# First batch's softmax turned by TensorE through PSUM, with a new order in the opening, and four side units moved

## The chip, the cores and the metric

The kernel runs on one core of a Trainium2 chip. Its time is the device time of one execution in microseconds (us), and the kernel before has a median of 645.45 us over three runs (644.94 to 646.62). Five engines work side by side, each through its own instructions in order: TensorE (PE, matrix products into the eight banks of PSUM, with its weight loads shown as PEld), VectorE (DVE), ScalarE (ACT), GpSimd (POOL) and SyncE (SP), which issues most transfers.

## The reference

Attention in both directions between 512 tokens and 32 state rows per head (8 batches, 8 heads, 64 wide), then one feed-forward layer over all 4,608 rows:

```
scores = x @ state.T / 8 ;  a  = softmax(scores)  ;  xread = a @ state    (tokens read the state)
scores2 = state @ x.T / 8 ; a2 = softmax(scores2) ;  sread = a2 @ x           (state reads the tokens)
X = rows of [xread, sread], 512 wide (8 heads x 64)
h = X @ w_in (512 x 2048) ;  g = h - tanh(h) ;  out = g @ w_out (2048 x 512)
```

The two weights arrive as 64-bit floats, and the kernel makes 32-bit ones of them itself.

## The kernel before

**Folding.** xread is never formed. For each batch the kernel builds M = (the states of 8 heads) times w_in, which is 256 x 2048, so that h = a M: per slice f of 128 columns of w_in there is a "hidden" product into a PSUM bank `hps`, tanh on ACT, the difference on DVE, and the "output" product into four banks `ops` (one per 128 tokens). Batches are called chunks, 0 to 7; chunk 8 is sread. A main loop of 64 steps (one step is one slice f of one of chunks 0 to 3, hidden two steps ahead) lets `ASIDE`, a table of step numbers, hang side work on the steps: `"att3"` is the attention of batch 3 in pieces, `"m0"` runs `m_units`, whose 16 units build M for batches 2 to 7. Batch 0's outputs are made in two halves: the first half's sums are stored and read back at step 29 as four tiles `part0` to `part3` (`load_partial`), and added at step 31, the end of chunk 0, by four DVE adds, `ob` (L587).

**The ring c2.** Tiles with the tag `c2` share four slots in turn: the copies `sl` that each unit of `m_units` makes and sends out by four transfers (`late`, L249), the four `part` tiles, and the last two of the four `ob` tiles of a chunk's store (`tag, bufs = ... ("c2", CSB)`). Who gets a slot waits until its last holder has been read.

**The opening.** Chunk 0 cannot start before its softmax, its M and its weights are there. This first stretch is written out by hand as a string of letters, `SEQ`; each becomes instructions, and each engine keeps this order. The digit is a half j of batch 0 (512 columns) or a weight block. S: scores (PE, bank `sps`). c: copy to `s` (ACT). T: turn to tokens on partitions. M, B, E, Z, N: maximum, subtraction (DVE), exponential (ACT), sum, division (DVE). A: turn back, giving `at`. Between them the weights are converted: a, b (DVE), r (ACT), p (DVE) turn a 64-bit block into 32-bit values. m: M's product (PE, bank `mps`). k and R: the copies (ACT) of the two halves of `mps`, for batch 0 (`m_first`) and batch 1 (`m_second`). h and H: the two halves of a hidden product (PE). X, x: tanh and difference. D: a product of zeros (`warm <- blank`) whose result nobody reads. In the kernel before, T and A are DVE transposes in blocks of 32x32.

After `SEQ` a scheduler sets the order on each engine from the order of the code and its own costs. Blocks 4 and 5 of the weights are rows 0 and 1 of w_out (r4, r5, p4, p5); after p5 DVE converts w10, w11, w02, w12 and w13 and splits row 2 of w_out into a high and a low part (L104, `wo`); PE needs the low part for the products of L566.

Of the kernel before, what the change touches and what calls it, by code (L numbers as in the profile page):

```python
# [9 lines left out]
F32 = mybir.dt.float32  # L10
# [6 lines left out]
AX = mybir.AxisListType  # L17
# [3 lines left out]
P = 128  # L21
B, H, S, NS, D = 8, 8, 512, 32, 64
# [16 lines left out]
def attention_ffn(ctx: ExitStack, tc: tile.TileContext, xT, xn, bd, bh, sp, sm, sl, win, wout, xout, tout, sout):  # L39
# [10 lines left out]
    nc = tc.nc  # L50

    cpool = ctx.enter_context(tc.tile_pool(name="cpool", bufs=1))
    pool = ctx.enter_context(tc.tile_pool(name="pool", bufs=2))
    dram = ctx.enter_context(tc.tile_pool(name="dram", bufs=1, space=DRAM))
    ps_o = ctx.enter_context(tc.tile_pool(name="ps_o", bufs=4, space=PSUM))
# [12 lines left out]
    TB = int('3')  # L68
    RRB = int('1')
    PTB = int('2')  # L70
    ident = cpool.tile([P, P], F32, name="ident")
    make_identity(nc, ident)
    wo = {}
    wod = dram.tile([P, 2, 2, NFF // 2, 2, 256], F32, name="wod")
# [13 lines left out]
    def bank(p, name):  # L88
        return p.tile([P, 512], F32, tag=p.name, name=name)
# [7 lines left out]
    def big(name, shape, dtype):  # L97
        return pool.tile(shape, dtype, tag="big", name=name, bufs=BIG)
# [7 lines left out]
    class Weight:  # L106
# [5 lines left out]
        def load(self):  # L112
            if self.src.dtype == F32:
                self.raw = next(raws)(f"{self.name}d", [P, 512], F32)
                dst = self.raw
            else:
                self.raw = next(raws)(f"{self.name}d", [P, 512, 2], U32)
                dst = self.raw.rearrange("p f w -> p (f w)")
            src = self.src.bitcast(dst.dtype)
            if len(src.shape) == 3:  # L120
                dst = dst.rearrange("p (r f) -> p r f", r=4)
            loadlog.append(nc.sync.dma_start(dst, src).ins)
# [19 lines left out]
        def convert(self, dst):  # L142
            return [step() for step in self.steps(dst)][1].ins
# [14 lines left out]
    def second(q):  # L158
        return pool.tile([P, 2, 512], F32, tag="stage", name=f"mr1{q}", bufs=SB)
# [438 lines left out]
    ats = [None] * 2  # L598
# [53 lines left out]
    def o(x):  # L652
        tc.keep_in_program_order(x)
        if x.ins.engine == mybir.EngineType.DVE:
            firstDVE[0] = x.ins
# [9 lines left out]
    nc.sync.dma_start(sps, sp)  # L665
    load(3)

    blank = pool.tile([P, 512], F32, tag="t", name="blank", bufs=TB)
    nc.gpsimd.memset(blank, 0.0)
    warm = bank(ps_a, "warm")  # L670
    m_first[0] = pool.tile([P, 2, 512], F32, tag="mr", name="mr00", bufs=RRB)
    wb, mps, sps_ps, hps, ss = {}, {}, {}, {}, {}
    es, ms, zs = {}, {}, {}
    csteps = {}
    hts = {}
    PING = int('0')
# [3 lines left out]
    def e3(hf):  # L680
        return es[hf].rearrange("p (a n) -> p a n", n=32)

    def step(op):
        k, j = op[0], int(op[1]) if len(op) > 1 else 0
        if k == "D":
            o(nc.tensor.matmul(warm[:, :256], blank[:, :P], blank[:, :256], start=True, stop=True))
        elif k == "S":
            sps_ps[j] = bank(ps_o, f"sps0{j}")
            for c in range(2):
                o(nc.tensor.matmul(sps_ps[j][64 * c : 64 * c + 64], bdr[:, 2 * j + c], xrs[j][:, c], start=True, stop=True))  # L690
        elif k == "c":
            if j == 0:
                kept[0] = pool.tile([P, 2, 512], F32, tag="g", name="s0", bufs=GB)
            ss[j] = kept[0][:, j]
            o(nc.scalar.copy(ss[j], sps_ps[j]))
        elif k == "T":
            es[j] = pool.tile([P, 512], F32, tag="e", name=f"e0{j}")
            o(nc.vector.transpose(es[j], ss[j]))
        elif k == "M":
            ms[j] = pool.tile([P, 16, 1], F32, tag="m1", name=f"m10{j}")  # L700
            o(nc.vector.reduce_max(ms[j], e3(j), axis=AX.X))
        elif k == "B":
            o(nc.vector.tensor_sub(e3(j), e3(j), ms[j].broadcast_to([P, 16, 32])))
        elif k == "E":
            o(nc.scalar.activation(es[j], es[j], AF.Exp, scale=SCALE))
        elif k == "Z":
            zs[j] = pool.tile([P, 16, 1], F32, tag="z", name=f"z0{j}")
            o(nc.vector.reduce_sum(zs[j], e3(j), axis=AX.X))
            o(nc.vector.tensor_scalar_add(zs[j], zs[j], EPS))
            o(nc.vector.reciprocal(zs[j], zs[j]))  # L710
        elif k == "N":
            o(nc.vector.tensor_mul(e3(j), e3(j), zs[j].broadcast_to([P, 16, 32])))
        elif k == "A":
            ats[j] = pool.tile([P, 512], F32, tag="p2t", name=f"at0{j}", bufs=PTB)
            o(nc.vector.transpose(ats[j], es[j]))
        elif k in "abrp":
            if j not in csteps:
                if j > 3:
                    if j == 4:
                        plain[0] = big("wp0", [P, 2, DM], F32)  # L720
                    csteps[j] = wos[j - 4].steps(plain[0][:, j - 4])
                else:
                    if j % 2 == 0:
                        wb[j // 2] = pool.tile([P, 2, 512], F32, tag="wf", name=f"w00{j}", bufs=WB)
                    csteps[j] = w0[0][j].steps(wb[j // 2][:, j % 2])
            o(csteps[j]["abrp".index(k)]())
            if k == "p":
                load(1)
            if k == "p" and j < 4:
                w = wb[j // 2][:, j % 2].rearrange("p (r f) -> p r f", r=4)  # L730
                nc.sync.dma_start(wf[0][:, :, j * P : j * P + P], w)
        elif k == "m":
            w = wb[j // 2][:, j % 2].rearrange("p (r f) -> p r f", r=4)
            mps[j] = bank(MP[j], f"mps0{j}").rearrange("p (r f) -> p r f", r=4)
            for p in range(4):
                o(nc.tensor.matmul(mps[j][:, p], sps[:, p], w[:, p], start=True, stop=True))
        elif k == "k":
            for c in range(2):
                o(nc.scalar.copy(m_first[0][64 * c : 64 * c + 64, :, j * P : j * P + P], mps[j][0:64, c::2]))
        elif k in "hH":  # L740
            if k == "h":
                hps[j] = bank(ps_h, f"hps0_{j}")
            i = "hH".index(k)
            o(nc.tensor.matmul(hps[j], m_first[0][:, i, j * P : j * P + P], ats[i], start=(i == 0), stop=(i == 1)))
        elif k == "X":
            t = hts[j] = pool.tile([P, 512], F32, tag="t", name=f"t0_{j}", bufs=TB)
            hts[j, 0] = nc.scalar.activation(t, hps[j], AF.Tanh)
            o(hts[j, 0])
        elif k == "x":
            g = chunks[0].g[j] = pool.tile([P, 512], F32, tag="g", name=f"g0_{j}", bufs=GB)  # L750
            d = nc.vector.tensor_sub(g, hps[j], hts[j])
            o(d)
            tanhs.append((hts[j, 0].ins, d.ins))
        elif k == "R":

            if 0 not in m_second:
                m_second[0] = second(0)
            for c in range(2):
                o(nc.scalar.copy(m_second[0][64 * c : 64 * c + 64, :, j * P : j * P + P], mps[j][64:128, c::2]))

    MP = [{"a": ps_a, "o": ps_o}[x] for x in 'oaoa']
    SEQ = 'S0 a0 c0 r0 b0 D D S1 T0 p0 M0 m0 a1 c1 B0 E0 T1 r1 b1 M1 k0 p1 D D D m1 B1 k1 r2 Z0 a2 N0 b2 D D D A0 E1 Z1 h0 p2 N1 R0 h1 A1 r4 r3 m2 R1 a3 H0 b3 k2 X0 H1 X1 p3 m3 x0 k3 R3 a4 x1 b4 R2 p4 a5 r5 b5 p5'
    for op in SEQ.split():
        step(op)
    chunks[0].m[0] = [m_first[0][:, k] for k in range(2)], None
    a0 = state_read(0, ss)
    late1 = late_read(1)
    turn = firstDVE[0]
    for p in range(2):
# [6 lines left out]
    m1 = m_units()  # L776
# [4 lines left out]
        "first": [18],  # L781
        "att2": [17, 18, 19, 22, 23, 25, 26, 27, 28],
        "part": [29],
        "m0": [17, 18, 19, 20, 22, 23, 24, 25, 26, 27, 28, 29, 30, 31, 33, 34],
        "att3": [29, 30, 30, 31, 32, 33, 34, 35, 36],
        "a0": [37, 38, 38, 39],
        "att5": [39, 40, 40, 41, 42, 43, 44, 45, 46],
# [262 lines left out]
    for n, duo in enumerate(duos):  # L1050
        a, b = duo.a.i, duo.b.i
# [112 lines left out]
```

## Time and profile before

| | us |
|---|---|
| median of three runs | 645.45 (644.94 to 646.62) |
| the profiled execution, whole | 646.61 |
| its span, first to last instruction | 644.8 |
| PE busy | 630.7 (98%) |
| DVE busy | 474.9 (74%) |
| ACT busy | 386.5 (60%) |

A span is what the profiler saw; the device time has 1.8 us around it. PE is busy nearly all the time, so time can be won or lost mainly where PE stands still, and the rows further down are of these places. A product of two 32-bit operands is two records on PE, so "x4" may be two products.

### The profile page before, as it was taken

The numbers are of one execution on the slowest core, as the hardware profiler recorded it, in microseconds if no ns is written. First come the engines' busy times: TensorE is split into PE (matmuls) and PEld (weight loads), VectorE is DVE, ScalarE is ACT, GpSimd is POOL, SyncE is SP. The second block draws the span as 40 slices with busy tenths as digits, with TensorE's granted clock in tenths as the row PEclk, the third lists the DMA queues.
The fourth block names the chain that finished last, engine by engine and source line by source line (L and its number), as shares of the span: only waits on it lengthen the run. The fifth ranks groups of instructions, "written<-read, shape, count | busy, mean of one in ns | idle before, by whom it ended". The sixth has DMA issues, their size and how long they took to land.

```text
span 644.8 us, 9604 instructions
## 1 busy us (share of the span) xinstructions
PE 630.7 (98%) x3448; PEld 485.8 (75%) x3448; DVE 474.9 (74%) x769; ACT 386.5 (60%) x667; POOL 24.4 (4%) x39
## 2 busy tenths in 40 slices
PE   6999999999998999999999999999999999999997
PEld 3445777777775788778878887788888888888996
DVE  5989998577556975999439777997955789754542
ACT  4874899668666765676546675456655553543432
POOL 0000000000000000000000000000000000333300
PEclk9999999999999999999999999999999999999999
DMA  9993964768897866679951446474565536999800
GB/s 316 293 372 119 350 201 174 221 159 280 264 292 239 291 215 213 209 241 350 384 210 36 161 132 228 136 228 156 169 177 165 189 113 188 301 319 340 274 23 33
DMA packets 67439, 141.21 MB, mean 219 GB/s; under 512 B 6976, under 2 KB 28736, under 8 KB 67392
## 3 DMA queue, kind: packets, MB, share of 16 engines
q1 hardware_dynamic: 64688, 132.08, 62.5%
q0 software_dynamic: 2560, 8.39, 3.8%
q8 instruction: 27, 0.44, 0.3%
q14 instruction: 20, 0.16, 0.1%
q10 hardware_dynamic: 144, 0.13, 0.1%
HBM read 96.01 MB, written 44.56 MB: 218 GB/s over the span
## 4 chain that ended last, share of the span: by engine, by line
PE 90%; DVE 3%; DMA 3%; ACT 1%; SPq 1%; issue 1%; DVEq 0%; ACTq 0%
PE X L999 13%; PE hps L509 10%; PE ops L565 9%; PE hps L510 9%; PE ops L567 9%; PE hps L511 9%; PE ops L566 9%; PE Y1m L999 5%; PE Y0m L999 4%; PE ops L563 2%; PE mps L240 2%; PE mls L247 2%; PE rps L455 1%; DMA w01d<-in_win 1%; PE hps L507 1%; PE pps L434 1%
## 5 line engine op out<-in xcount | busy, mean ns | idle before, releaser
L509 PE MATMUL hps<-aT,m 128*128 128x512 f32 x240 | 95.9, 402 | 0.3 <-DVE G L524 0.2
L510 PE MATMUL hps<-aT,m 128*128 128x512 f32 x240 | 93.8, 391 | 0.0
L511 PE MATMUL hps<-aT,m 128*128 128x512 f32 x240 | 93.4, 390 | 0.0
L565 PE MATMUL ops<-wo,g 128*128 128x512 f32 x232 | 91.1, 397 | 1.7 <-DVE ob L587 1.7
L566 PE MATMUL ops<-wo,g 128*128 128x512 f32 x232 | 90.7, 391 | 0.6 <-DVE wo L104 0.6
L567 PE MATMUL ops<-wo,g 128*128 128x512 f32 x232 | 84.5, 393 | 0.0
L530 DVE TENSOR_TENSOR t<-hps,t 128x512 f32<-128x512 f32 (+1 forms) x74 | 46.6, 630 | 39.6 <-ACT t L530 39.0
L524 ACT ACTIVATE t<-hps 128x512 f32<-128x512 f32 x64 | 38.3, 598 | 62.5 <-PE hps L511 60.0
L524 DVE TENSOR_TENSOR G<-hps,t 128x512 f32<-128x512 f32 x64 | 43.9, 687 | 36.4 <-ACT t L524 36.3
L530 ACT ACTIVATE t<-hps 128x512 f32<-128x512 f32 (+1 forms) x74 | 40.8, 551 | 46.0 <-PE hps L511 45.4
L104 ACT CAST g<-t 128x512 fp32r<-128x512 f32 (+1 forms) x74 | 42.4, 574 | 27.2 <-DVE t L530 26.9
L104 DVE TENSOR_TENSOR g<-t,g 128x512 fp32r<-128x512 f32 (+1 forms) x74 | 46.7, 631 | 16.0 <-ACT g L104 15.8
L565 PEld LDWEIGHTS ops<-wo,g 128*128 128x128 f32 x232 | 43.4, 188 | 18.8 <-DVE ob L587 2.2
L509 PEld LDWEIGHTS hps<-aT,m 128*128 128x128 f32 x240 | 45.1, 188 | 15.0 <-DVE G L524 2.1
L511 PEld LDWEIGHTS hps<-aT,m 128*128 128x128 f32 x240 | 45.1, 188 | 9.5
L510 PEld LDWEIGHTS hps<-aT,m 128*128 128x128 f32 x240 | 45.1, 188 | 9.1 <-issue 0.2
L566 PEld LDWEIGHTS ops<-wo,g 128*128 128x128 f32 x232 | 43.6, 188 | 10.6 <-DVE wo L104 1.0
L567 PEld LDWEIGHTS ops<-wo,g 128*128 128x128 f32 x232 | 43.2, 188 | 11.0 <-DVE wo L104 0.8
L999 PE MATMUL X<-g0m,W0m 128*128 128x512 f32 x192 | 46.6, 389 | 0.0
L104 ACT CAST g1m<-G 128x1024 fp32r<-128x1024 f32 x28 | 29.5, 1056 | 28.0 <-PE Y1m L999 11.9
L1037 POOL DMA_DIRECT2D wl<-wod x32 | 23.3, 728 | 587.7 <-DMA W1m<-wsd 556.6
L999 PE MATMUL X<-g1m,W1m 128*128 128x512 f32 x192 | 45.3, 389 | 0.0
(263 smaller groups left out, 1159.0 us busy)
## 6 DMA issues: line engine op xcount, KB each, us to landing
mr<-md SPq DMA_DIRECT2D x26, 512.0 KB, 4.0
xT<-in_xT SPq DMA_DIRECT2D x16, 512.0 KB, 6.1
md<-st SPq DMA_DIRECT2D x64, 128.0 KB, 2.6
xn<-in_xn SPq DMA_DIRECT2D x16, 512.0 KB, 5.6
wsd<-ws SPq DMA_DIRECT2D x16, 512.0 KB, 4.2
wod<-wo SPq DMA_DIRECT2D x32, 256.0 KB, 6.1
W0m<-wsd SPq DMA_DIRECT2D x16, 512.0 KB, 3.8
W1m<-wsd SPq DMA_DIRECT2D x16, 512.0 KB, 4.3
```

What stands on the lines that cost most here:

```text
L104: return nc.scalar.copy(hi, src), (sub or nc.vector).tensor_sub(lo, src, hi)
L240: made = nc.tensor.matmul(pss[e], s0[rows, x, 2 * p + e], t[rows, y], start=(n == 0), stop=(n == 2))
L509: nc.tensor.matmul(ps, mhi[k][:, cols], ahi[:, k], start=(k == 0), stop=False)
L510: nc.tensor.matmul(ps, mhi[k][:, cols], alo[:, k], start=False, stop=False)
L511: made = nc.tensor.matmul(ps, mlo[k][:, cols], ahi[:, k], start=False, stop=(k == nk - 1))
L524: main(nc.scalar.activation(t, ps, AF.Tanh), nc.vector.tensor_sub(g, ps, t))
L530: tanhs.append((nc.scalar.activation(t, ps, AF.Tanh).ins, nc.vector.tensor_sub(t, ps, t).ins))
L565: nc.tensor.matmul(o, g[:, 0, tok], w[:, 0], start=(f in self.begins), stop=False)
L566: nc.tensor.matmul(o, g[:, 0, tok], w[:, 1], start=False, stop=False)
L567: return nc.tensor.matmul(o, g[:, 1, tok], w[:, 0], start=False, stop=stop).ins
L999: made = nc.tensor.matmul(out[t], w[:, e, x, cols], y[:, e], start=first and j == 0 and e == 0 and c == 0, stop=last and j == 3 and e == 1 ...
L1037: nc.gpsimd.dma_start(wo[f][:, :, cols].bitcast(F32), wod[:, f % 2, half, f // 2])
```

## The change

Four edits. T becomes four PE transposes of 128x128 into a bank `tps`, from which M and B read; the subtraction B writes `e` in SBUF. A becomes four PE transposes into a bank `aps`, and a new letter y copies that to `at` on ACT. The sum's two small instructions get a letter of their own, z. `SEQ` is written anew: four D stand first, with `blank` now 256 wide and set by DVE at the very start, and three more D stand later (eight before, seven now). In `ASIDE`, `"m0"` leaves steps 29, 30 and 31; the 16 units now stand at 17 to 28 without a gap and at 32 to 35.

```
+    blank = pool.tile([P, 512], F32, tag="t", name="blank", bufs=TB)[:, :256]
+    nc.vector.memset(blank, 0.0)
     make_identity(nc, ident)
...
-    blank = pool.tile([P, 512], F32, tag="t", name="blank", bufs=TB)
-    nc.gpsimd.memset(blank, 0.0)
...
         elif k == "T":
-            es[j] = pool.tile([P, 512], F32, tag="e", name=f"e0{j}")
-            o(nc.vector.transpose(es[j], ss[j]))
+            tps[j] = bank(ps_o, f"tps0{j}")
+            for t in range(4):
+                cols = slice(P * t, P * t + P)
+                o(nc.tensor.transpose(tps[j][:, cols], ss[j][:, cols], ident))
         elif k == "M":
...
-            o(nc.vector.reduce_max(ms[j], e3(j), axis=AX.X))
+            o(nc.vector.reduce_max(ms[j], tps[j].rearrange("p (a n) -> p a n", n=32), axis=AX.X))
         elif k == "B":
-            o(nc.vector.tensor_sub(e3(j), e3(j), ms[j].broadcast_to([P, 16, 32])))
+            es[j] = pool.tile([P, 512], F32, tag="e", name=f"e0{j}")
+            s3 = tps[j].rearrange("p (a n) -> p a n", n=32)
+            o(nc.vector.tensor_sub(e3(j), s3, ms[j].broadcast_to([P, 16, 32])))
...
         elif k == "A":
+            aps[j] = bank(ps_o, f"aps0{j}")
+            for t in range(4):
+                cols = slice(P * t, P * t + P)
+                o(nc.tensor.transpose(aps[j][:, cols], es[j][:, cols], ident))
+        elif k == "y":
             ats[j] = pool.tile([P, 512], F32, tag="p2t", name=f"at0{j}", bufs=PTB)
-            o(nc.vector.transpose(ats[j], es[j]))
+            o(nc.scalar.copy(ats[j], aps[j]))
...
-    SEQ = 'S0 a0 c0 r0 b0 D D S1 T0 p0 M0 m0 a1 c1 B0 E0 T1 r1 b1 M1 k0 p1 D D D m1 B1 k1 r2 Z0 a2 N0 b2 D D D A0 E1 Z1 h0 p2 N1 R0 h1 A1 r4 r3 m2 R1 a3 H0 b3 k2 X0 H1 X1 p3 m3 x0 k3 R3 a4 x1 b4 R2 p4 a5 r5 b5 p5'
+    SEQ = 'D D D D S0 a0 r0 b0 p0 c0 T0 S1 M0 c1 B0 D a1 b1 E0 r1 T1 Z0 m0 M1 k0 D z0 N0 B1 D A0 p1 E1 y0 m1 k1 a2 Z1 h0 r2 b2 z1 r3 N1 h1 A1 p2 y1 m2 a3 k2 b3 p3 H0 X0 H1 X1 m3 r4 x0 k3 R0 R1 R3 a4 x1 b4 R2 p4 a5 r5 b5 p5'
...
-        "m0": [17, 18, 19, 20, 22, 23, 24, 25, 26, 27, 28, 29, 30, 31, 33, 34],
+        "m0": [17, 18, 19, 20, 21, 22, 23, 24, 25, 26, 27, 28, 32, 33, 34, 35],
```

Where the instructions stand: first ACT at the start of the kernel, before (`s` are c0 and c1, `w00r` is r0, `e` is E0).

```order
L695 ACT_TABLE_LOAD
L695 COPY s_143<-sps_137 128x512
L138 ACTIVATE w00r<-w00d 128x512
L695 COPY s_143<-sps_149 128x512
L705 ACTIVATE e_152<-e_152 128x512
```

The same engine and place in the changed kernel.

```order
L140 ACT_TABLE_LOAD
L140 ACTIVATE w00r<-w00d 128x512
L695 COPY s_153<-sps_141 128x512
L695 COPY s_153<-sps_160 128x512
L710 ACTIVATE e_166<-e_166 128x512
```

The first copy of the scores now stands behind the conversion r0 of the first weight block.

Next ACT from the copy k2 to r5 and beyond, before (`t_0`, `t_1` are X0 and X1, `mr_136` copies are k, `mr_220` copies are R, `wo0r` is r4 and stands further up, `wo1r` is r5).

```order
L138 ACTIVATE wo0r<-wo0d 128x512
L138 ACTIVATE w03r<-w03d 128x512
L759 COPY mr_220<-mps_185 64x2x128 x2
L739 COPY mr_136<-mps_232 64x2x128 x2
L747 ACTIVATE t_0_244<-hps_0_213 128x512
L747 ACTIVATE t_1_247<-hps_1_223 128x512
L739 COPY mr_136<-mps_253 64x2x128 x2
L759 COPY mr_220<-mps_253 64x2x128 x2
L759 COPY mr_220<-mps_232 64x2x128 x2
L138 ACTIVATE wo1r<-wo1d 128x512
L138 ACTIVATE w10r<-w10d 128x512
```

The same place in the changed kernel (`mr_274` copies are R).

```order
L750 COPY mr_136<-mps_243 64x2x128 x2
L758 ACTIVATE t_0_257<-hps_0_221 128x512
L758 ACTIVATE t_1_260<-hps_1_230 128x512
L140 ACTIVATE wo0r<-wo0d 128x512
L750 COPY mr_136<-mps_262 64x2x128 x2
L770 COPY mr_274<-mps_181 64x2x128 x2
L770 COPY mr_274<-mps_209 64x2x128 x2
L770 COPY mr_274<-mps_262 64x2x128 x2
L770 COPY mr_274<-mps_243 64x2x128 x2
L140 ACTIVATE wo1r<-wo1d 128x512
L140 ACTIVATE w10r<-w10d 128x512
```

Between the second tanh and r5 (`wo1r`) stood three pairs of copies; now r4 (`wo0r`) and five pairs stand there.

Last DVE at the end of chunk 0, before (the adds `ob_20` and `ob_30`; `e` and `m` belong to the attention of batch 3).

```order
L104 TENSOR_TENSOR g_2_2095<-t_2_2092,g_2_2095 128x512
L370 STREAM_TRANSPOSE e_1987<-s_1983 128x512
L411 TENSOR_REDUCE m_2184<-s_1983 128x1
L370 STREAM_TRANSPOSE e_1993<-s_1985 128x512
L411 TENSOR_REDUCE m_2246<-s_1985 128x1
L587 TENSOR_TENSOR ob_20_2079<-ops_8_2_1532,part_1879 128x512
L372 TENSOR_REDUCE m_1989<-e_1987 128x16
L530 TENSOR_TENSOR t_3_2143<-hps_3_2136,t_3_2143 128x512
L413 TENSOR_SCALAR nm_2186<-m_2184 128x1
L587 TENSOR_TENSOR ob_30_2082<-ops_8_3_1533,part_1881 128x512
```

The same place in the changed kernel.

```order
L589 TENSOR_TENSOR ob_00_2032<-ops_8_0_1575,part_1920 128x512
L106 TENSOR_TENSOR ws_2104<-wa_2096,ws_2103 128x1024
L589 TENSOR_TENSOR ob_10_2035<-ops_8_1_1576,part_1922 128x512
L532 TENSOR_TENSOR t_2_2051<-hps_2_2044,t_2_2051 128x512
L589 TENSOR_TENSOR ob_20_2038<-ops_8_2_1577,part_1924 128x512
L589 TENSOR_TENSOR ob_30_2041<-ops_8_3_1578,part_1926 128x512
L106 TENSOR_TENSOR wst_2143<-w_2057,wst_2143 128x512
L106 TENSOR_TENSOR g_2_2054<-t_2_2051,g_2_2054 128x512
```

All four adds now stand ahead of the attention of batch 3 and within six instructions of each other.

## Rows read from the trace of the kernel before

**Rows 1.** The page: PE's busy time, share of the span, instructions; other engines after it.

```profile
PE 630.7 (98%) x3448; PEld 485.8 (75%) x3448; DVE 474.9 (74%) x769; ACT 386.5 (60%) x667; POOL 24.4 (4%) x39
```

**Rows 2.** PE's waits: line, for whom, us in total, times, longest.

```profile
PE sps L690 <- DMA xT<-in_xT: 4.7, 1, 4.7
PE ops L565 <- DVE ob L587: 1.7, 1, 1.7
PE hps L744 <- DVE at L715: 1.2, 1, 1.2
PE mps L736 <- DMA sps<-in_sp: 0.9, 1, 0.9
PE ops L566 <- DVE wo L104: 0.6, 1, 0.6
```

**Rows 3.** PE in the opening: start, length in us, instructions [idle before, releaser].

```profile
4.71 1.98 PE L690 MATMUL sps<-xT,bdr 128*64 128x512 f32 x4 [4.71 <-DMA xT<-in_xT]
...
8.62 1.08 PE L690 MATMUL sps<-xT,bdr 128*64 128x512 f32 x4
...
13.00 1.16 PE L736 MATMUL mps<-w,sps 128*128 128x128 f32 x8
...
19.48 1.98 PE L744 MATMUL hps<-at,mr 128*128 128x512 f32 x4
...
35.38 0.50 PE L566 MATMUL ops<-wo,g 128*128 128x512 f32 x1 [0.58 <-DVE wo L104]
```

**Rows 4.** One stretch by engine: busy us (instructions), granted clock, DMA share, GB/s.

```profile
5.00:9.00 4.00, 4.00 (x10) 1.38 (x9) 1.98 (x5) 1.27 (x2) 0.00 (x0) 1.00 1.05 368
```

**Rows 5.** DVE in the opening, columns as in rows 3.

```profile
7.02 0.43 DVE L136 TENSOR_SCALAR w<-w00d 128x512 uint32<-128x512 uint32 x1 [7.02 <-DMA w00d<-in_win]
...
7.71 0.69 DVE L698 STREAM_TRANSPOSE e<-s 128x512 f32<-128x512 f32 x1
...
10.12 0.69 DVE L703 TENSOR_TENSOR e<-e,m 128x512 f32<-128x512 f32 x1
...
14.38 0.25 DVE L710 RECIPROCAL z<-z 128x16 f32<-128x16 f32 x1
...
14.83 0.68 DVE L712 TENSOR_TENSOR e<-e,z 128x512 f32<-128x512 f32 x1
...
21.27 0.69 DVE L751 TENSOR_TENSOR g<-hps,t 128x512 f32<-128x512 f32 x1 [0.35 <-ACT t L747]
...
25.50 0.69 DVE L139 CUSTOM_DVE_ANT_0 wp<-wp,wo1r 128x1024 uint16<-128x1024 uint16 x1 [0.81 <-ACT wo1r L138]
...
34.62 0.71 DVE L104 TENSOR_TENSOR wo<-wor,wo 128x512 fp32r<-128x512 f32 x1
```

**Rows 6.** ACT in the opening.

```profile
6.72 0.59 ACT L695 COPY s<-sps 128x512 f32<-128x512 f32 x1 [4.70 <-PE sps L690]
7.20 0.79 ACT L138 ACTIVATE w00r<-w00d 128x512 uint16<-128x512 uint32 x1
...
10.85 0.63 ACT L705 ACTIVATE e<-e 128x512 f32<-128x512 f32 x1 [0.51 <-DVE e L703]
...
21.50 0.60 ACT L747 ACTIVATE t<-hps 128x512 f32<-128x512 f32 x1 [0.26 <-PE hps L744]
...
23.16 1.51 ACT L759 COPY mr<-mps 64x256 f32<-64x256 f32 x4
24.69 0.78 ACT L138 ACTIVATE wo1r<-wo1d 128x512 uint16<-128x512 uint32 x1
```

**Rows 7.** POOL at the start: the zeros of `blank`.

```profile
0.88 0.53 POOL L669 MEMSET blank<- 128x512 f32 x1
```

**Rows 8.** PE: transposes of 128x128 in a later attention, eight of them.

```profile
173.59 1.03 PE L434 MATMUL pps<-ident,s 128*128 128x128 f32 x8
```

**Rows 9.** DVE at the end of chunk 0: the late add.

```profile
208.11 0.69 DVE L587 TENSOR_TENSOR ob<-ops,part 128x512 f32<-128x512 f32 x1 [2.69 <-DMA md<-sl]
```

**Rows 10.** PE in the same stretch: its two waits.

```profile
197.66 0.96 PE L247 MATMUL mls<-wst,sls 128*128 128x512 f32 x3 [0.46 <-ACT sl L249]
...
208.85 0.50 PE L565 MATMUL ops<-wo,g 128*128 128x512 f32 x1 [1.74 <-DVE ob L587]
```

More of the change, by code (lines that the diff above doesn't have):

```diff
@@ L672, in attention_ffn @@
     wb, mps, sps_ps, hps, ss = {}, {}, {}, {}, {}
-    es, ms, zs = {}, {}, {}
+    es, ms, zs, tps, aps = {}, {}, {}, {}, {}
     csteps = {}
@@ L685, in step @@
         if k == "D":
-            o(nc.tensor.matmul(warm[:, :256], blank[:, :P], blank[:, :256], start=True, stop=True))
+            o(nc.tensor.matmul(warm[:, :256], blank[:, :P], blank, start=True, stop=True))
         elif k == "S":
@@ L708, in step @@
             o(nc.vector.reduce_sum(zs[j], e3(j), axis=AX.X))
+        elif k == "z":
             o(nc.vector.tensor_scalar_add(zs[j], zs[j], EPS))
```

## The prediction

> **What bounds the kernel now.** I read the page's busy shares first: PE is busy for 630.7 us, 98% of the span [rows 1]. Work that DVE or ACT loses or gains therefore counts only where PE stands still for it. PE's waits, read next, name five such places of 0.5 us or more that this change comes near [rows 2]: 4.7 us for the first token block, 0.9 for `sps`, 1.2 for `at`, 0.6 for the low part of a w_out row, and 1.7 for an add `ob`. The first four lie before 36 us, the last at 208.85 us. Then I read the opening engine by engine [rows 3, 5, 6]. The reader should see that two chains decide it. PE waits for `at` early on, but at 35.38 it waits for DVE again (L104, `wo`), and there DVE is the late one: it has run without a pause since p5 at 25.50, and p5 itself had waited 0.81 us for ACT's r5 (`wo1r`), which started at 24.69. Whatever moves r5 moves PE's restart at 35.38.
>
> The clock: at 4.71 the two products of S0 take 1.98 us, at 8.62 the same two of S1 take 1.08 [rows 3]. [...]
>
> **The change part by part: the opening.** It takes four transposes of 0.69 us from DVE [rows 5], 2.8 us, adds sixteen transposes on PE and two copies of 0.59 [rows 6] on ACT, and reorders all three engines. The sum must follow the chain. An instruction on DVE or ACT starts about 0.1 us before the end of the one ahead (c0 at 6.72 lasts to 7.31, r0 starts at 7.20), and one that waits for another engine starts 0.03 to 0.06 after it.
>
> The unknown prices. *PE transposes*: eight took 1.03 us [rows 8] with about 0.1 between starts, so four take some 0.6; at the least 0.5, at the most the 1.16 of m1's four products of the same 128 columns [rows 3]. I take 0.6. *DVE reading PSUM*: x0 reads a bank and takes 0.69, B0 in SBUF 0.69 [rows 5], so nothing either way; I allow 0.05 up or down for each of four. *The zeros on DVE*: POOL needed 0.53 for twice the width [rows 7], so between 0 and 0.53 after about 0.74. A blank of 256 columns at the low level costs at most half of S0's 1.98, so four end by 1.27 + 3.96 = 5.2, and S0 by 7.2 even at that level. The cover is r0: c0 now stands behind it on ACT, and r0 waits for the block that lands at 7.02 [rows 5]. So the faster S0 and the early blanks gain nothing: c0 starts at 7.70 instead of 6.72.
>
> From there, at the high level: c0 ends at 8.29, T0 runs 8.35 to 8.95, M0 to 9.66, B0 to 10.36, E0 (0.63) to 11.0. DVE then goes through Z0, M1, the two small ones (0.25 and less), N0, B1 and p1; at 0.6 from start to start, and 0.5 for the small pair, p1 starts at 11.05 + 2.9 = 13.9 and ends at 14.6. That lets m1 start at 14.65, against 13.00 [rows 3]. m1 ends at 15.8, k1 (half of 1.51 [rows 6]) at 16.55, r2 (0.79) at 17.35, p2 at 18.05, m2 leads to H0 at 19.05 against 19.48. The second tanh, X1, follows H0 by 2.02 as before, so it starts at 21.05 instead of 21.50. Up to here the new order is 0.4 us ahead.
>
> Then it loses this. Between X1 and r5 ACT had three pairs of copies, now it has r4 and five pairs: 0.5 for X1, 0.65 for r4, five times 0.755 [rows 6], so r5 starts at 21.05 + 0.5 + 0.65 + 3.8 = 26.0, against 24.69. Of its 0.78 the end is at 26.8, p5 starts there instead of at 25.50, and DVE's list behind it (w10 to the low part of row 2) is the same work as before. So `wo` at 34.62 comes 1.3 us later, and PE restarts at 36.7 instead of 35.38. The time DVE was spared is idle time in front of p5. The list of waits names none of PE between there and 197 us in which this could be made good. Opening: **+1.3 us**; from the bounds above -0.4 to +2.1 (T0 at its dearest adds 0.56, the four reads 0.2; the low end is p5 no later than before, and PE ahead by the 0.4 of H0).
>
> [...]
>
> **The change part by part: steps 29 to 31.** The add `ob_20` starts at 208.11 after DVE has idled 2.69 us for a transfer `md<-sl` [rows 9], and PE idles 1.74 us for it [rows 10]. In the ring of four, `part0` to `part3` hold all slots and the copies `sl` of the units at 29 to 31 come between them and the adds, so an add must wait until an `sl` has been sent. With no unit at 29 to 31 the next holders of the slots are the adds themselves, which wait for the adds before them on their own engine. PE's 1.74 goes. The 0.46 at 197.66 is a product `mls` that waits for ACT to empty the bank of the unit just before; three units' products stood within ten microseconds there, now they do not: it goes too. What is late next: the banks of chunk 2's output, freed by four adds that stand within six instructions on DVE, some 4 us in all at 0.6 to 1.2 each. Between the last product of chunk 0 and the first of chunk 2 PE has nine products of a unit, about 2.9 us at 0.96 for three [rows 10], and it takes the four banks one after the other, each for six products or more, 1.9 us at that price; the adds need at most 1.2 + 0.6 us from one bank to the next and so keep ahead. The four units at 32 to 35 bring 4 x 9 products that PE had to do anyway. Steps: **-2.2 us**; between -2.2 and, if as much waiting returns at 32 to 35, 0.
>
> **The sum.** +1.3 - 1.74 - 0.46 = -0.9 us. On the profiled execution that is 646.61 - 0.9 = 645.7. That execution lies 1.16 above the median of the three, so for the median I say 645.45 - 0.9 = **644.5 us**. About 0.3%, 1.9 us, is what a measurement of this kernel tells from no change; 643.5 and 647.4 are the bounds.
>
> **The rivals.**
>
> *A. r5 is not late.* For this: DVE has 2.8 us less to do, and H0 is 0.4 us ahead. Against: five pairs at 0.755 each are counted from rows, and ACT is in order. If p5 starts at 25.5 or earlier, DVE's list ends with PE's own pace, PE keeps up to its lead of 0.4 and loses up to its 0.58 of waiting, and the sum is -2.2 to -3.2: about -2.6, **642.9**. Chance 0.20.
>
> *B. The clock stays low (slower).* PE does its blanks from 1.2 to 5, S0, then nothing until c0 is there at 8.3, and then transposes, short products and waits, where before it worked without a stop from 5 to 9 us [rows 4]. [...] Against: the level held over the waits of 0.9 and 1.2 us in the opening [rows 2]; the new pause of 2.3 us is longer than any row shows. Chance 0.11.
> [...] No row here shows a transpose at the low level.
>
> *C. The wait at the end of chunk 0 moves.* The units at 32 to 35 meet the attention of batch 3 and the mixing of w_out rows on DVE. If 1.5 to 2.2 us come back there, the sum is +0.6 to +1.3: **646.4**. For it: DVE has the four adds in a row and a unit's split in each of these steps. Against: before, with DVE as loaded, PE's list of waits names no other place than these two between 36 and 350 us. Chance 0.15.
>
> **How the numbers follow.** The forecast has 0.54, with its own range 643.6 to 645.6; A 0.20, B 0.11, C 0.15. Faster by over 0.3%: A and a little of the forecast's low end, 0.22. Slower: B and a rest of C, 0.13. Within: 0.65. The range runs from A's 642.7 to 647.3; outside it lie B and the lowest part of A, some 0.18 together.
>
> **What would show it.** After the change, r5 on ACT near 26.0 and p5 on DVE near 26.8 with 2 to 3 us of idle time before it; PE's wait for `wo` near 36.7, about 2 us long; h of the first hidden product before 16.6, H0 near 19.0; no wait of DVE for `md<-sl` and none of PE for `ob` near 208; S1's two products at about 1.1 us. The prediction is wrong if r5 starts before 25, if m1 takes 2 us instead of 1.16, or if new waits of PE stand between 185 and 235 us.

## The result and the profile after

The changed kernel takes 650.74 us (median of six runs, 648.53 to 651.54) against 645.66 of the kernel before (six runs). The ratio is 1.006, with a 95% interval of 1.0043 to 1.0076: 0.6% slower, 3.9 us. The two medians lie 5.1 us apart, more than the ratio says; comparisons below go by the ratios unless they name a median. The forecast was 644.5, its range 642.7 to 647.3. The profiled execution took 651.54 us, its span is 649.4.

PE's waits in the changed kernel come first: who waited, for whom, us in total, times, longest. They answer to [rows 2].

```profile
PE tps L701 <- ACT s L695: 2.9, 1, 2.9
PE ops L568 <- DVE wo L106: 1.9, 1, 1.9
...
PE hps L511 <- DVE t L532: 0.6, 1, 0.6
...
PE mps L242 <- ACT st L207: 0.5, 1, 0.5
...
```

The waits for `ob` and `mls` are gone. The wait for `wo` (now L568) has grown from 0.58 to 1.88 us, a pause of 2.9 us stands in front of the first transposes, and two waits that did not exist, for `st` and `t`, stand near 218 and 221 us.

PE in the opening of the changed kernel (start, length, instructions [idle before, releaser]), to be held against [rows 3]:

```profile
4.90 1.15 PE L690 MATMUL sps<-xT,bdr 128*64 128x512 f32 x4
8.96 1.08 PE L701 MATMUL tps<-ident,s 128*128 128x128 f32 x4 [2.91 <-ACT s L695]
9.97 1.98 PE L690 MATMUL sps<-xT,bdr 128*64 128x512 f32 x4
...
12.63 0.66 PE L701 MATMUL tps<-ident,s 128*128 128x128 f32 x4
...
38.90 0.55 PE L568 MATMUL ops<-wo,g 128*128 128x512 f32 x1 [1.88 <-DVE wo L106]
39.24 0.63 PE L569 MATMUL ops<-wo,g 128*128 128x512 f32 x1
...
44.24 1.09 PE L187 MATMUL mps<-w,sps 64*32 64x512 f32 x16
```

Two lines of the kernel before go with the last three; they follow the restart at 35.38 in [rows 3]:

```profile
35.72 0.39 PE L567 MATMUL ops<-wo,g 128*128 128x512 f32 x1
...
39.16 1.09 PE L185 MATMUL mps<-w,sps 64*32 64x512 f32 x16
```

The reader is to compare equal work. S0 at 4.90 takes 1.15 us and the same S1 at 9.97 takes 1.98; four transposes take 1.08 at 8.96 and 0.66 at 12.63; a product behind the wait at 38.90 takes 0.63 where it took 0.39 to 0.50 before. PE had got its full clock and lost it twice. The granted clock says so (busy us per engine as in [rows 4], the figure behind the engines is the clock):

```profile
5.00:8.40 3.40, 1.05 (x4) 0.17 (x4) 0.80 (x2) 0.80 (x2) 0.00 (x0) 1.00 1.00 354
8.50:11.90 3.40, 2.94 (x9) 1.03 (x9) 2.48 (x5) 0.31 (x1) 0.00 (x0) 0.50 1.08 372
...
36.00:39.00 3.00, 1.12 (x5) 0.59 (x4) 3.00 (x7) 2.73 (x6) 0.00 (x0) 1.00 1.02 385
39.30:42.60 3.30, 3.30 (x9) 2.58 (x8) 2.48 (x6) 1.74 (x3) 0.00 (x0) 0.50 0.99 264
```

Twice the granted clock is 0.50; S1 there takes 1.98 us, the length of S0 in the kernel before [rows 3], and this pace is the prediction's low level. The first fall lies between 8.40 and 8.50 us, while PE was still standing in its pause of 2.91 us: the first transpose starts only at 8.96. The second lies between 39.0 and 39.3 us, just behind the pause of 1.88 us. In the kernel before, the record of the clock begins at 8.65 us and is at 1.00 up to 643.5 us; so the 1.00 of [rows 4] says nothing of the time before 8.65, in which S0 took its 1.98 us.

Last, ACT and then DVE in the changed kernel:

```profile
7.60 0.78 ACT L140 ACTIVATE w00r<-w00d 128x512 uint16<-128x512 uint32 x1 [5.58 <-DMA w00d<-in_win]
8.25 0.56 ACT L695 COPY s<-sps 128x512 f32<-128x512 f32 x1
11.99 0.58 ACT L695 COPY s<-sps 128x512 f32<-128x512 f32 x1 [3.18 <-PE sps L690]
12.47 0.63 ACT L710 ACTIVATE e<-e 128x512 f32<-128x512 f32 x1
...
25.15 3.04 ACT L770 COPY mr<-mps 64x256 f32<-64x256 f32 x8
28.21 0.78 ACT L140 ACTIVATE wo1r<-wo1d 128x512 uint16<-128x512 uint32 x1
```

```profile
10.80 0.69 DVE L708 TENSOR_TENSOR e<-tps,m 128x512 f32<-128x512 f32 x1
...
29.03 0.69 DVE L141 CUSTOM_DVE_ANT_0 wp<-wp,wo1r 128x1024 uint16<-128x1024 uint16 x1 [2.45 <-ACT wo1r L140]
...
38.17 0.67 DVE L106 TENSOR_TENSOR wo<-wor,wo 128x512 fp32r<-128x512 f32 x1
```

The subtraction B0 ends at 11.49, but E0 stands on ACT behind c1, and c1 waits for the slow S1 until 11.99. That is how a slow product gets onto the chain. And r5 (`wo1r`) starts at 28.21, behind all four pairs R, so p5 at 29.03 has waited 2.45 us.

**The bill of the profiled executions.** The span grew by 4.5 us (649.37 against 644.85). PE's restart at the low part of `wo` moved from 35.38 to 38.90: +3.5. From that restart to the first products of the next M (L187, before L185), the same work takes 44.24 - 38.90 = 5.34 instead of 39.16 - 35.38 = 3.78: +1.56, the second stretch at half clock. The waits near 200 us are 1.09 instead of 2.20. What is then left of the 4.5 us, 0.56, is by difference and has no cause that was looked for.

### The profile page after: what moved, and what is told of

The parts are those of the page before. It is cut to its first block, busy times and chain, and to the rows that moved or that the text cites. A ratio compares the mean times of both kernels' runs of the same rounds, so it can differ in the third digit from the quotient of the medians.

```text
span 649.4 us, 9631 instructions
## 1 busy us (share of the span) xinstructions
PE 636.2 (98%) x3462; PEld 488.9 (75%) x3462; DVE 473.4 (73%) x766; ACT 386.9 (60%) x669; POOL 24.0 (4%) x38
## 4 chain that ended last, share of the span: by engine, by line
PE 90%; DVE 4%; ACT 2%; DMA 2%; issue 1%; SPq 1%; DVEq 0%; ACTq 0%
PE X L1010 13%; PE hps L511 10%; PE hps L512 9%; PE hps L513 9%; PE ops L567 9%; PE ops L568 9%; PE ops L569 9%; PE Y1m L1010 5%; PE Y0m L1010 4%; PE ops L565 2%; PE mps L242 2%; PE mls L249 2%; PE rps L457 1%; PE sps L348 1%; PE hps L509 1%
## 5 line engine op out<-in xcount | busy, mean ns | idle before, releaser
L568 PE MATMUL ops<-wo,g 128*128 128x512 f32 x232 | 91.4, 394 | 1.9 <-DVE wo L106 1.9
L532 DVE TENSOR_TENSOR t<-hps,t 128x512 f32<-128x512 f32 (+1 forms) x74 | 46.6, 630 | 38.3 <-ACT t L532 37.7
L568 PEld LDWEIGHTS ops<-wo,g 128*128 128x128 f32 x232 | 44.0, 190 | 11.2 <-DVE wo L106 2.3
```

Of the source, the lines that this page charges most:

```text
L532: tanhs.append((nc.scalar.activation(t, ps, AF.Tanh).ins, nc.vector.tensor_sub(t, ps, t).ins))
L568: nc.tensor.matmul(o, g[:, 0, tok], w[:, 1], start=False, stop=False)
```

## The experiments

All were timed in five rounds beside the kernel before; "clock" is the mean granted clock of an execution. By the profiled executions, 0.996 or 0.997 is one stretch of 0.50 of the length shown above (3.4 us); 0.995 is two of them (the changed kernel) or one of twice the length (e4, e8); 0.999 and 1.000 are none but at the very end. Parts of a line that are left out of an edit are marked with three dots.

**e1: the side units' new steps alone, in the kernel before.**

```
-        "m0": [17, 18, 19, 20, 22, 23, 24, 25, 26, 27, 28, 29, 30, 31, 33, 34],
+        "m0": [17, 18, 19, 20, 21, 22, 23, 24, 25, 26, 27, 28, 32, 33, 34, 35],
```

> The kernel before with the new steps of the side units alone. Theory: the waits for ob (1.74) and mls (0.46) go, and two smaller ones come back at steps 32 to 35 (0.52 for st, 0.57 for t, as in the changed kernel's trace): -1.1 us, about 644.4, clock 1.00 throughout. Rival 1 (the units are part of the loss): the units' new steps cost as much as they save or more: 645.5 to 647. Rival 2 (the record's own step): -2.2 us, 643.3.

Measured: 647.35 us, ratio 1.0019 (1.0009 to 1.0029), slower by 1.2 us; rival 1 is right. Every execution has a mean clock of 0.999 or 1.000, so the clock has no part in this loss. PE's waits for `ob` and `mls` are gone; these two, at 214.71 and 217.26 us, are new:

```profile
PE mps L240 <- ACT st L205: 1.2, 1, 1.2
...
PE hps L509 <- DVE t L530: 0.6, 1, 0.6
```

Why they stand there is to be seen on ACT in e1:

```profile
212.64 1.05 ACT L104 CAST m<-mr 128x1024 fp32r<-128x1024 f32 x1 [4.86 <-DMA mr<-md]
213.59 1.06 ACT L205 COPY st<-mps 128x512 f32<-128x512 f32 x2
...
215.07 0.61 ACT L530 ACTIVATE t<-hps 128x512 f32<-128x512 f32 x1
```

ACT stands at the cast of chunk 2's M for 4.86 us, waiting for its transfer, and the copies `st` of the unit at step 32 and the tanh stand behind it in order. SP's issues in e1:

```profile
204.18 1.38 SPq L424 DMA_DIRECT2D xn<-in_xn  x2
205.61 0.42 SPq L271 DMA_DIRECT2D mr<-md  x1
```

and the same transfer in the kernel before:

```profile
198.46 0.61 SPq L271 DMA_DIRECT2D mr<-md  x1
```

The load of M went out 7 us earlier there, ahead of the two `xn` blocks. The two sums of waits (2.20 before, 1.8 in e1) do not explain the loss of 1.2 us. But the profiled execution of the kernel before, 1.16 us above the median of its three, may not be typical of the old steps. Two other kernels that keep them, e7 and e8 below, wait 0.51 and 0.74 us for `ob` instead of 1.74; this is e8's line:

```profile
PE ops L567 <- DVE ob L589: 0.7, 1, 0.7
```

From PE's restart in the opening to the end of the span, the kernel before takes 609.47 us, e7 608.57 and e8 608.47, and e1 609.95. Against e7 and e8, whose openings differ from e1's, e1 loses 1.4 us there, close to what was measured; 0.6 to 0.8 us of it are its longer waits near 200 us, and the cause of the rest stays open.

**e2: the new opening alone** (the changed kernel with the old steps of the units; the diff is e1's, turned round).

> The changed kernel with the old steps of the side units: the opening alone. Theory: the opening carries the whole loss, 3.5 us of later restart at L568 and 1.6 us in the stretch of half clock behind it, so about 645.5 + 5.2 = 650.7 plus or minus 1, with two stretches of granted clock 0.50 near 8.5 and 39 us; slower than the changed kernel by the 1.1 us that the units bring, 651.8 at most. Rival (the units are part of the loss): 648 or less.

Measured: 648.54 us, ratio 1.0052 (1.0037 to 1.0067), slower by 3.4 us, less than the theory's 5.2 and near its rival's bound. Five executions have a mean clock of 0.997; the sixth has 1.000 and is the slowest of all, 650.86, so the clock is not the only thing that varies here. The profiled one is instructive, since in it the clock had risen late (at 7.32 us) and did not fall behind the first pause, 1.58 us here. PE:

```profile
8.46 0.63 PE L701 MATMUL tps<-ident,s 128*128 128x128 f32 x4 [1.58 <-ACT s L695]
9.02 1.08 PE L690 MATMUL sps<-xT,bdr 128*64 128x512 f32 x4
...
37.05 0.50 PE L568 MATMUL ops<-wo,g 128*128 128x512 f32 x1 [1.88 <-DVE wo L106]
```

The restart is 37.05, as against 38.90 with the first stretch at half clock. So the first stretch, with a weight block that came 0.5 us later, costs up to 1.85 us, and the opening's order by itself 1.67. Units and opening together: 1.0019 x 1.0052 = 1.0071, inside the interval of the whole change.

**e3: PE's first pause filled.**

```
- D D D D S0 a0 r0 ...
+ D D D D S0 D D D D D a0 r0 ...
```

> The changed kernel with five more products of zeros between S0 and T0, where PE paused for 2.91 us; nothing else differs. Theory (the clock fell because of the pause): no stretch of 0.50 near 8.5 us, T0's four transposes 0.65 instead of 1.08 us, S1 1.1 instead of 1.98, c1 some 1.2 us earlier and E0 behind it too, restart of PE at L568 near 37.7 instead of 38.9; the second wait of 1.9 us stays, with a stretch of 0.50 behind it: -1.2 us, about 649.5. Rival 1 (transposes do not hold the clock up whatever is done before them): T0 and S1 as long as before, a stretch of 0.50 between 8 and 13 us, no gain: 650.7. Rival 2 (the first stretch is covered by other waits): the clock stays at 1.00 but the restart is still near 38.9: 650.7.

Measured: 650.80 us (649.14 to 653.31), ratio 1.0081 (1.0063 to 1.0099): no gain in the median. The profiled execution, the fastest, has T0 at 0.63 and S1 at 1.08 us, restarts at 37.28 and took 649.14 us, near the theory's 37.7 and 649.5; but it has no stretch of 0.50 at all, not even behind its wait of 1.88 us for `wo`, where the theory had one. The other five have 0.996 or 0.997. Since PE takes its list in order, T0 stands behind five products. Their ten records took 2.43 us here; at the start, nearly all of it ahead of 4.83 us, where the record of the clock begins, eight such records took 3.78 us. From these two I estimate nearly twice the 2.43 us wherever the clock is still low, and take this for the reason that the others gain nothing, but no run measured it. The experiment settles nothing on the median.

**e4: r5 ahead of the copies R.**

```
- ... x0 k3 R0 R1 R3 a4 x1 b4 R2 p4 a5 r5 b5 p5
+ ... x0 k3 r5 R0 R1 R3 a4 x1 b4 R2 p4 a5 b5 p5
```

> The changed kernel with r5 ahead of the four pairs of copies R on ACT, nothing else. Theory: r5 starts near 25.2 instead of 28.2, p5 on DVE near 26.6 instead of 29.0, the wait of 1.88 us for wo at 38.90 falls to 0.5 or less, and with it goes the second stretch of 0.50 near 39 to 42.6: -1.4 to -1.9 for the wait and -1.6 for the clock, about 647.4. Rival 1 (the wait goes, the clock stays low for another reason): about 649. Rival 2 (the copies R, now 0.65 later, or another step of DVE's list are late in its place): the restart stays near 38.5 or later: 650.3 to 651.

Measured: 647.50 us, ratio 1.0018 (1.0004 to 1.0032): 2.7 us better than the changed kernel by the ratios, 3.2 by the medians. On ACT, DVE and PE:

```profile
24.85 0.79 ACT L140 ACTIVATE wo1r<-wo1d 128x512 uint16<-128x512 uint32 x1
```
```profile
26.41 0.69 DVE L141 CUSTOM_DVE_ANT_0 wp<-wp,wo1r 128x1024 uint16<-128x1024 uint16 x1
```
```profile
36.12 0.39 PE L568 MATMUL ops<-wo,g 128*128 128x512 f32 x1
36.35 0.39 PE L569 MATMUL ops<-wo,g 128*128 128x512 f32 x1
```

No wait for `wo`, and no stretch of 0.50 behind it. PE is at 36.12 although the clock in this execution was 0.50 from 7.85 to 14.68 us; that fall, too, lies within the first pause (2.62 us, up to 8.40). Six of the seven executions have 0.995 or 0.997; the one with 0.999 took 644.96 us.

**e5: c0 ahead of r0 again.**

```
- ... S0 a0 r0 b0 p0 c0 T0 ...
+ ... S0 a0 c0 r0 b0 p0 T0 ...
```

> The changed kernel with c0 (the first copy of the scores) ahead of r0 on ACT again, nothing else. Theory (the pause of 2.9 us before T0 pulls the clock down and holds up the chain): c0 starts near 6.1 instead of 8.25, the pause before T0 falls below 1.2 us, no stretch of 0.50 near 8.5 us, S1 takes 1.1 us, m1 starts near 14.5 instead of 16.78; the second wait of about 1.9 us for wo stays, with a stretch of 0.50 behind it: restart at L568 near 36.8, -2 us against the changed kernel, about 648.7. Rival 1 (transposes and short products do not hold the clock up, with or without the pause): a stretch of 0.50 before 15 us all the same, 650 or more. Rival 2 (c0 was not on the path): T0 starts no earlier than 8 us, 650.7.

Measured: 648.25 us, ratio 1.0035 (1.0022 to 1.0048), 1.6 us better than the changed kernel by the ratios, whose intervals just overlap, and 2.5 by the medians. PE:

```profile
7.15 0.63 PE L701 MATMUL tps<-ident,s 128*128 128x128 f32 x4 [0.78 <-ACT s L695]
8.01 1.08 PE L690 MATMUL sps<-xT,bdr 128*64 128x512 f32 x4 [0.23 <-DMA xT<-in_xT]
...
36.21 0.62 PE L568 MATMUL ops<-wo,g 128*128 128x512 f32 x1 [1.89 <-DVE wo L106]
36.63 0.63 PE L569 MATMUL ops<-wo,g 128*128 128x512 f32 x1
```

With a pause of 0.78 us the transposes and S1 run at full clock; the wait of 1.89 us for `wo` is still there, and 0.50 follows it (36.45 to 39.86). In the profiled executions pause and low clock go together in both places, one place at a time: e4 takes away the second, e5 the first. But a pause does not always bring it: four of e5's nine executions have a mean clock of 1.000 and took 647.29 to 648.25 us, the other five have 0.996 or 0.997 and took 647.77 to 649.72.

**e8: four zero products first, in the kernel before, its softmax still turned by DVE.**

```
- S0 a0 c0 r0 b0 D D S1 ...
+ D D D D S0 a0 c0 r0 b0 S1 ...
```

> The kernel before with four zero products at the very start (two of them new, two taken from behind S0; zeros set by DVE), its softmax still turned by DVE. It tells what the early products alone do to the clock. Theory: the granted clock is 1.00 from about 5 to 7 us on, S0 takes 1.1 to 2.0 us, and PE pauses for some 1 to 2 us between S0 and S1, which by chance of the instant pulls the clock down again in some executions: 645.0 to 646.5, with some executions at a mean clock of 0.997. Rival 1 (an early clock is a gain): S0 and the chain behind it 0.8 us earlier, 644.7. Rival 2 (the early products alone make the loss of the changed kernel): 648 or more.

Measured: 647.11 us (644.91 to 648.92), ratio 1.0012 (0.9998 to 1.0026), which is not told from no change. Eleven of twelve executions have a clock of 0.997 or less; the one with 1.000 is the fastest, 644.91. PE in the profiled one, and the granted clock:

```profile
8.45 1.08 PE L690 MATMUL sps<-xT,bdr 128*64 128x512 f32 x4 [1.74 <-DMA xT<-in_xT]
10.77 2.05 PE L736 MATMUL mps<-w,sps 128*128 128x128 f32 x8 [1.23 <-DMA sps<-in_sp]
```
```profile
9.90:16.60 6.70, 5.83 (x21) 5.33 (x22) 6.60 (x14) 2.31 (x5) 0.00 (x0) 0.50 1.06 382
```

There is no transpose on PE here, and the clock falls all the same, behind the pause of 1.74 us and within that of 1.23 (up to 10.77). In the kernel before, where PE began only with the data and worked on from there, waits of 0.9 and 1.16 us [rows 2] came after 8.65, and the clock stayed at 1.00.

**e6: the units at 17 to 28 and 33 to 36, in the kernel before** (none at 32).

> The kernel before with the sixteen units at 17 to 28 and 33 to 36, none at 32. Theory (at 32 the unit's copies st on ACT stand behind the cast of M, which waits 4.9 us for its transfer): without a unit at 32 the wait of 1.24 us for st goes, and with ob and mls gone too it is 1.2 to 2 us faster than the units at 32 to 35: 645.3 to 646.2, the kernel before's time or a little less. Rival 1 (the wait goes to another instruction behind the same cast, such as t, or the unit at 33 waits as long): 647 or more. Rival 2 (the record's step, no wait left): 643.3 to 644.

Measured: 645.41 us, ratio 0.9989 (0.998 to 0.9997): 0.7 us faster than before, about 2 us better than e1. The load of M goes out earlier again, the cast waits less, and nothing that PE needs stands behind it:

```profile
200.18 0.50 SPq L271 DMA_DIRECT2D mr<-md  x1
```
```profile
205.68 1.05 ACT L104 CAST m<-mr 128x1024 fp32r<-128x1024 f32 x1 [3.38 <-DMA mr<-md]
```

PE's waits for `ob`, `mls`, `st` and `t` are all gone. It is the gain that the prediction hoped for from the units, one step further on, but a third of its 2.2 us. From PE's restart to the end e6 takes 607.72 us, 0.8 us less than e7 and e8 with the old steps, close to the measured gain.

**e7: the changed opening mended, old steps of the units.**

```
- ... S0 a0 r0 b0 p0 c0 T0 S1 M0 c1 B0 D a1 ...
+ ... S0 a0 c0 D r0 b0 p0 T0 D S1 M0 c1 B0 a1 ...
- ... E1 y0 m1 ...
+ ... E1 y0 R0 m1 ...
- ... x0 k3 R0 R1 R3 a4 x1 b4 R2 p4 a5 r5 b5 p5
+ ... x0 k3 r5 R1 R3 a4 x1 b4 R2 p4 a5 b5 p5
```

> The changed kernel's opening mended at four places (c0 ahead of r0; one zero product each before T0 and S1; r5 ahead of three pairs of copies; R0 right behind y0) with the old steps of the units. Theory: no pause of PE over 1.3 us after S0, no stretch of 0.50 in any part of the opening, restart at L568 near 33.9 to 34.4 against 35.38 of the kernel before: -1 to -1.5 us against before, 644.1 to 644.6. Rival 1 (transposes let the clock fall): a stretch of 0.50 before 15 us, 646 to 648. Rival 2 (another chain of DVE or ACT sets the restart): 645.5 with the clock at 1.00.

Measured: 645.02 us, ratio 0.9988 (0.9978 to 0.9998), every execution at 0.999 or 1.000. PE restarts without a wait:

```profile
34.29 0.40 PE L568 MATMUL ops<-wo,g 128*128 128x512 f32 x1
```

With sixteen transposes on PE, and no pause above 0.69 us between the zero products and this line, the clock holds.

**e9: e7's opening and e6's units.**

> The mended opening (as in e7) with the units at 17 to 28 and 33 to 36 (as in e6). Theory (the two are independent, since they lie 150 us apart): the ratios multiply, 0.9988 x 0.9989 = 0.9977, about 644.2 at a kernel before of 645.7; restart at L568 near 34.2, no wait of PE over 0.4 us between 36 and 300 us, no stretch of 0.50. Rival (the units' good place depended on the old opening's timing, or the order of the transfers shifts): one of the waits for st, ob or mls is back, 645 or more.

Measured: 644.11 us (643.69 to 644.17), ratio 0.9964 (0.9951 to 0.9977), the best of all: it beats both kernels, by a little more than the forecast of 0.9977. PE's waits in e9; none lies between 36 and 300 us:

```profile
...
PE sps L690 <- DMA xT<-in_xT: 0.7, 1, 0.7
PE tps L701 <- ACT s L695: 0.7, 1, 0.7
PE aps L723 <- DVE e L718: 0.6, 1, 0.6
PE sps L348 <- ACT sr L207: 0.5, 1, 0.5
PE mps L747 <- DVE w L141: 0.5, 1, 0.5
PE hps L511 <- DVE G L526: 0.4, 1, 0.4
```

**e10: the softmax turned by DVE, r5 early, e6's units** (the kernel before with `x0 k3 r5 R3 a4 x1 b4 R2 p4 a5 b5 p5` at the end).

> The kernel before, its softmax still turned by DVE, with r5 ahead of the copies R3 and R2 on ACT, and the units at 17 to 28 and 33 to 36. It tells whether the transposes on PE are worth anything once the rest is mended. Theory: p5's wait of 0.81 us and PE's 0.58 at L566 go, restart near 34.9; 0.4 us better than the units alone (0.9989): about 0.9983, 644.6, some 0.4 us behind the mended opening with transposes on PE. Rival 1 (the wait for wo stays, DVE being the late one without r5's wait): 645.0. Rival 2 (the turn on DVE costs nothing at all): level with or ahead of e9.

Measured: 644.79 us (644.31 to 647.19, the last at a mean clock of 0.95, which stays unexplained), ratio 0.9977 (0.9964 to 0.9989). The wait for `wo` is gone, PE is at 35.01. The intervals of e9 and e10 overlap, but the twelve executions all lie above e9's five: the new opening, once its order is mended, is worth some 0.7 us. That is the opening as a whole, since e9 and e10 differ in the early zero products and the rest of the order too; what the transposes alone bring no run shows.

## Why the prediction was wrong

**What bounds the kernel: right.** What was found to move the time were PE's own stops and PE's clock.

**The opening's chain: right in mechanism and nearly in size.** At full clock (e2) r5 starts at 26.36 and p5 at 27.17, where I had 26.0 and 26.8, and PE restarts at 37.05 where I had 36.7: +1.67 against my +1.3. The unknown prices held: four transposes take 0.60 to 0.66 at full clock (I took 0.6), and M0 and B0, which read PSUM, take 0.69 each, as Z0 and N0 do from SBUF (all e2). e4 confirms r5's place as the cause.

**The clock: one of two steps that failed, by 2.1 us (+3.4 for the opening in e2, +1.3 forecast).** It was rival B, with a chance of 0.11, but in another form. I asked whether PE would stay at the low level from the start. In fact, with the four zero products from 1.19 us on, the record begins at 1.00 already at 5.08 us (8.65 before), and the clock falls to 0.50 within the pause that the new order makes in front of T0. I counted that pause (I wrote 2.3 us, it was 2.9), but set it only against waits of 0.9 and 1.2 us that the level had held over; nothing among my rows covered a pause twice as long, and there I should have given the rival more. And I priced only the opening. The wait for `wo`, which I forecast at about 2 us and counted once, also had a fall of the clock behind it, for another 1.56 us. The bounds of the opening (-0.4 to +2.1) held no term for either; the runs show up to 1.85 and 1.56 us.

**Who pulled it down: the pauses, not the transposes.** The first fall in the changed kernel comes before its first transpose (8.96 us), in e8 the clock falls without one on PE, and in e7 and e9, with sixteen of them, every execution has a mean clock of 0.999 or 1.000. What transposes by themselves do to the clock, next to products, no run separates.

**Steps 29 to 31: the other step that failed, by 3.4 us.** It was right that the two waits go, wrong that 2.2 us are won: +1.2 was measured (e1). First, the size. I read 2.20 us of waits in one execution, 1.16 us above the median, and took them off the median. In e2, e7 and e8, with the same steps, the two waits come to 0.74, 0.97 and 1.20 us, and e6, in which they go and none comes back, gains 0.7. How long they are in a usual execution of the kernel before was not measured. Second, what is late next: I looked at the banks of chunk 2's output, and it was ACT, standing in order at the cast of chunk 2's M, with `st` and the tanh behind it. Rival C had the place (32 to 35) and nearly the size (1.5 to 2.2 us; 1.8 in e1), but named DVE. I had looked at DVE's order there and not at ACT's, nor at SP's, on which the load of M had moved behind `xn`. One of the signs I had named for being wrong, new waits of PE between 185 and 235 us, came; the other two, an early r5 and a slow m1, did not.

The sum then reads: +3.4 for the opening (e2) and +1.2 for the units (e1), 4.6, where +3.9 was measured (5.1 by the medians) and -0.9 forecast. Of the 5.5 us between 4.6 and the forecast, the steps make up 3.4 and the opening 2.1.

## What to carry to other kernels

A stop of the matrix engine had to be priced twice here: its own length (1.88 us for `wo`) and the half-clock work behind it (1.56 us more). Early filler products did not help where a long pause (2.91 us) came between them and the real work. A wait that is read in one execution is to be looked for in others before it is counted as a gain. Where a wait is removed by moving work, look on every in-order queue, the transfer queue too, at what the moved instructions now stand behind. Both order mistakes here (c0 behind r0, r5 behind the R copies) were single letters; mending them, together with zero products closer to the work and R0 earlier (e7), turned a loss of 3.4 us into a gain of 0.8.

## What the runs showed of the hardware

The clock fell within or behind pauses of 1.74 to 2.91 us (in e8 within one of 1.23 that followed soon after one of 1.74), and held over others (0.9, 1.16 and 1.74 before, 1.58 in e2, 1.88 in the profiled execution of e3). The length of the pause alone does not decide, then: behind 1.88 us the clock fell in the changed kernel and in e2 and not in e3. The instant at which it rises also differs between executions of like openings: with zero products from 1.19 us on, the record begins at 1.00 at 4.44 (e4), 4.83 (e3), 5.08 (changed), 6.41 (e8) and 7.32 us (e2). By the lengths of S0 this is the rise: 1.98 us where it ended ahead of that instant (e2 and the kernel before), 1.08 where it began behind it (e3, e4). So one profile shows one of several cases, and the mean clock of all runs has to be read beside it.
